# An mLSTM cell and a squared-ReLU FFN: squares moved to another engine, weights rounded two pieces at a time, odd chunks' attention put behind 64-row matmuls

## The chip, the cores and the metric

The kernel runs on one core of a Trainium2 chip. The core has a matrix engine (TensorE, PE in the profile), a vector engine (VectorE, DVE), an engine for functions of one argument (ScalarE, ACT), a general engine (GpSimd, POOL) and an engine that here only issues transfers (SyncE, SP). They run side by side, each in the order of its own instructions, and wait for each other through semaphores. SBUF is the on-chip memory, PSUM the memory that TensorE writes to, and transfers (DMA) run between DRAM and SBUF. The metric is the device time of one execution in microseconds (us), as a median over several runs.

## The reference

Two parts, one after the other. The first is an mLSTM cell: for 4 x 8 pairs of batch and head, 768 steps and a head size of 40, a matrix state and a vector state are decayed and added to at each step. The second is an FFN over 3072 tokens of width 320 with 2048 hidden units.

```python
for t in range(S):
    m_new = np.maximum(f_gate[:, :, t] + m, i_gate[:, :, t])
    f_stab = np.exp(f_gate[:, :, t] + m - m_new)
    i_stab = np.exp(i_gate[:, :, t] - m_new)
    m = m_new
    C = f_stab[:, :, None, None] * C + i_stab[:, :, None, None] * np.einsum('bhd,bhe->bhde', vt, kt)
    n = f_stab[:, :, None] * n + i_stab[:, :, None] * kt
    h_tilde = np.einsum('bhde,bhe->bhd', C, qt)
    nq = np.einsum('bhd,bhd->bh', n, qt)[:, :, None]
    denom = np.maximum(np.abs(nq), 1.0)
    o = 1.0 / (1.0 + np.exp(-o_gate[:, :, t]))
    y[:, :, t] = o * h_tilde / denom
x = y.transpose(0, 2, 1, 3).reshape(B * S, H * D)   # 3072 x 320
h = np.maximum(x @ w_in, 0.0)
out = h * h @ w_out
```

The FFN's weights come in as float64; the kernel makes float32 of them on the chip.

## The kernel before

Tokens are worked on in 24 chunks of 128 (`s` = 0 to 23; six chunks are one sequence, so chunks 0, 6, 12 and 18 start with no state). The recurrence is turned into attention inside a chunk, plus a state carried from chunk to chunk. Two chunks together make a group `g` of 256 tokens for the FFN, so there are 12 groups.

One chunk's attention is this series of steps. `load_A` brings a table of summed log decays, 512 KB, spread over all partitions, into one of two buffers. `decays` (ScalarE) makes exps of it that scale q (`scale_q`, VectorE); `mask` (POOL) blanks the future; `weigh` (ScalarE) makes eight exps, the weights; `values` (POOL) scales v for the state. `scores` (TensorE, L423) multiplies k by q with 40 rows of the array for each product, and `weighted` (VectorE, L438) multiplies scores by weights. `attend_turned` (L513, L522, L532) makes the numerator `numT` from the state and the weighted scores, and the state's increase `dC`; VectorE turns numT in blocks of 32 into `tn` and adds up the new state. Then the result goes twice through DRAM to get into the layout of the FFN: `store_num` (L551) writes `tn`, `load_num` (L556, four DMAs) reads it back, `normalise_turned` (VectorE) divides and applies the output gate, `store_rows` (L603) writes the rows, `load_rows` (L608, four DMAs) reads them as `xT`, and `turn_squares` (VectorE, L615) turns blocks of 32. `pair_up` (L289, four DMAs) and `load_squares` (L311, four DMAs) bring k and q of a later chunk in the layout for `scores`; `turn_kq` (L318) turns their blocks; `load` and `load_o` bring k, v and the output gate. All these DMAs are issued by SyncE, in the order in which the program has them.

The FFN's two products are done by a scheme with fewer multiplications (seven products of half blocks instead of eight) from group 3 on for the first product and from group 1 on for the second. `sums_of_x` (POOL) makes sums `xs` of the two chunks of a group. `ffn1_open` (L813) runs 32 matmuls: block X on xT of the group's first chunk, Y, V and Z on xs. `ffn1_close` runs 24 more over 128 rows (L813) and then 32 over 64 rows (L845), and VectorE and ScalarE join the four results; `ffn1_square` (ScalarE) takes rectifier and square in place. `ffn2_fast` (L739) is the second product in four steps of 32, 32, 32 and 16 matmuls.

The start is different. Until chunk 5 the weights are brought and rounded at the same time (`Rounding`: two reads by ScalarE, L196 and L198; three operations by VectorE, L207, L211 and L212; one add by POOL, L216). w_in takes 10 pieces of 512 columns, w_out 16 pieces of 320. Groups 0 to 2 go through `ffn1_main` and `ffn1_rest` (L645, L656), whose results `relu_half` (ScalarE, L671) writes into temporary tiles, and `square_half` (VectorE, L678) squares into the tile `g2` that the second product reads. Groups 0 and 1 are in the loop over `u`, group 2 is in the first four rounds of the main loop.

The order is written out by hand: no scheduler moves anything. The main loop (L1028) goes over quarters of chunks, `s, at = 6 + n // 4, n % 4`. Even chunks (from 8) carry the second product of group (s - 6) / 2, odd ones (from 9) the first product of group (s - 3) / 2, which holds chunks s - 3 and s - 2:

```python
    for n, (which, g, i) in enumerate(parts):
        s, at = 6 + n // 4, n % 4
        if at == 0:
            do(score, s)
        if at == 1:
            do(attend_turned, s)
```

So chunk o (odd) is attended to in its first two quarters, normalised and sent to DRAM in the third; the blocks of its xT are turned in the second quarter of chunk o + 1, `sums_of_x` reads them in its fourth, and `ffn1_open` in the first quarter of chunk o + 2.

Of the kernel before, what the change touches and what calls it, by code (L numbers as in the profile page):

```python
# [9 lines left out]
F32 = mybir.dt.float32  # L10
I32 = mybir.dt.int32
# [18 lines left out]
def kernel(  # L30
# [127 lines left out]
            ))  # L158
    IN_DONE = (3, 5, 8, 10)
    assert len(pieces) == IN_DONE[-1]  # L160
    pieces += [(w_out[:, fb, :], [(slice(0, P), wout_w[fb * P : (fb + 1) * P])]) for fb in range(NF)]
    NRAW = 4

    class Rounding:
# [11 lines left out]
        def fetch(self):  # L176
            n = len(self.raws)
            if n == len(pieces):
                return
            dst, srcs = pieces[n]  # L180
            raw = conv.tile([P, 512, 2], I32, name="raw", bufs=NRAW)
            self.raws.append(raw)
            for rows, src in srcs:
                to = raw[rows, : dst.shape[1]]
                if len(src.shape) == 4:
                    to = to.rearrange("p (a f) w -> p a f w", a=src.shape[1])
                nc.sync.dma_start(to, src)

        def words(self):
            n = len(self.a)  # L190
            if n == len(pieces):
                return
            w = pieces[n][0].shape[1]
            raw = self.raws[n][:, :w]
            mag = conv.tile([P, 512], F32, name="mag", bufs=3)
            nc.scalar.activation(mag[:, :w], raw[:, :, 1].bitcast(F32), AF.Abs)  # L196
            low = conv.tile([P, 512], F32, name="low", bufs=3)
            nc.scalar.activation(low[:, :w], raw[:, :, 0].bitcast(U32), AF.Copy, bias=2.0, scale=2.0 ** -51)  # L198
            self.a.append((mag, low))

# [464 lines left out]
    def relu_half():  # L665
        if "half" in st:
            hs, g4 = st.pop("half")
            rs = []
            for h in hs:
                rs.append(ffn.tile([P, 2, WG], F32, name="r_sb", bufs=4))  # L670
                nc.scalar.activation(rs[-1][:], h[:], AF.Relu)  # L671
            st.setdefault("relu", []).append((rs, g4))

    def square_half():
        if st.get("relu"):
            rs, g4 = st["relu"].pop(0)
            for i, r in enumerate(rs):
                nc.vector.tensor_tensor(g4[:, :, i, :], r[:], r[:], op=ALU.mult)  # L678

    def ffn2(g, j, part):  # L680
        if part == 0:
# [150 lines left out]

    def ffn1_close(g, q):
        xT, xs = st["xT", g], st["xs"]
        (X, Y, V, Z), (U2, U4) = st["f1"], st["U"]
        g4 = st["g2", g][:, 8 * q : 8 * q + 8, :].rearrange("p (n two) t -> p n two t", two=2)
        t0, t1 = slice(0, P), slice(P, 2 * P)
        blocks(X, F12, xT[:, 0, 1, :], q, False)
        blocks(Y, F21, xs[:, 2, :], q, True)
        blocks(V, WS[3], xT[:, 1, 1, :], q, True)  # L840
        lo, hi = slice(0, KR), slice(KR, 2 * KR)
        for pair in (((X, lo, xT[lo, 0, 2, :]), (Y, hi, xT[hi, 1, 2, :])), ((V, lo, xT[lo, 1, 2, :]), (Z, hi, xs[hi, 1, :]))):
            for n in range(4):
# [21 lines left out]
    def do(f, s):  # L865
        if 0 <= s < NT:
            f(s)
# [84 lines left out]
    rounding.step()  # L952


    NEXT = (5, 8, 10, 11, 13, 15, 17, 19)
    for u in range(8):
        s = 2 + u // 2
        relu_half()
# [63 lines left out]
    for g in range(1, NG):  # L1022
        parts += [(2, g, i) for i in range(4)]
        if g + 2 < NG:
            parts += [(1, g + 2, i) for i in range(4)]
    LAST = (21, 23, 25, 25, 26)
    assert LAST[-1] == len(pieces)
    for n, (which, g, i) in enumerate(parts):  # L1028
        s, at = 6 + n // 4, n % 4
        if n == 5:  # L1030
            brought.close()
            late = ctx.enter_context(tc.tile_pool(name="late", bufs=1, side="right"))
        if at == 0:
            do(score, s)
        if at == 1:
            do(attend_turned, s)
            do(decays, s + 1)
            do(mask, s + 1)
            if n > 4:
                do(turn_kq, s + 1)  # L1040
            do(decay_C, s + 1)
            if s > X_SQ:
                do(turn_squares, s - 1)
            do(store_num, s)
            do(load, s + 4)
            if 8 <= s < 20:
                load_o(s + 4)
            do(load_num, s)
            do(pair_up, s + 3)
        if 5 <= n < 8:  # L1050
            sums_of_weights(n - 5)
        if n == 6:
# [21 lines left out]
                for r in range(s + 1, min(s + 5, NT)):  # L1074
                    sigmoid(r)
        if fast:
            (ffn1_close if i % 2 else ffn1_open)(g, i // 2)
            if at == 2:
                do(scale_q, s + 1)
        elif which == 1:  # L1080
            ffn1_main(g, i)
            if i % 2 == 0:
                held = st["half"]
            else:

                both = held, st["half"]
                for more, half in enumerate(both):
                    ffn1_rest(g, i - 1 + more, half[0])
                for half in both:
                    st["half"] = half  # L1090
                    relu_half()
                    square_half()
        elif g == 0:
            ffn2(g, *divmod(i, 2))
        else:
            ffn2_fast(g, i)
        if at == 2:
            do(lambda s: weigh(s, masked=True), s + 1)
            ffn1_square()
            if n < 4:  # L1100
                do(turn_kq, s + 1)
                do(scale_q, s + 1)
            do(normalise_turned, s)
            do(store_rows, s)
            do(load_squares, s + 2)
            do(load_rows, s)
            do(load_A, s + 2)
        if at == 0:
            ffn1_square()
        if n < 5:  # L1110
# [32 lines left out]
```

## Time and profile before

| what | value |
|---|---|
| median of 11 runs | 517.78 us (516.82 to 519.33) |
| profiled execution, its own time | 518.15 us |
| its span in the profile | 516.4 us, 11946 instructions |
| TensorE busy | 505.2 us, 98% |
| VectorE, ScalarE, POOL busy | 367.7, 237.7, 113.7 us |
| TensorE busy from 0 to 127 us | 120.6 us |
| VectorE, ScalarE busy from 0 to 127 us | 104.5, 76.8 us |
| TensorE's granted clock, mean | 0.993 |
| DMA | 67.64 MB, 131 GB/s over the span |

The span runs from the first to the last instruction of one execution; the run's own time is a little longer. Busy time is given by engine. The chain of work that ended last follows the program back from its end, at each step to what released it. A list in order of time gives the start, the duration and how many instructions were merged; for a DMA it is the issue on the queue of the engine (SPq), not the transfer. Matmuls overlap, so in a merged row of the chain the duration divided by the count is the pace, shorter than one matmul's own time.

### The profile page before, as it was taken

What the parts mean: (1) busy time and instruction counts of PE and PEld (TensorE: products, weight loads), DVE (VectorE), ACT (ScalarE), POOL (GpSimd) and SP (SyncE); (2) the same over time, 40 slices, a digit from 0 to 9 for tenths busy, and PEclk for the clock granted to TensorE, in tenths of its full rate; (3) what the DMA queues carried; (4) which work ended last, traced back from release to release, by engine and by line L of the source; (5) the groups of instructions that cost most, each with busy time, mean ns of one, the idle gap of its engine ahead of it and who ended that gap; (6) DMA issues with size and microseconds to landing.
All of it is one profiled execution on the core that took longest, in us unless ns stands there. A gap on an engine that the chain in (4) does not pass through costs nothing.

```text
span 516.4 us, 11946 instructions
## 1 busy us (share of the span) xinstructions
PE 505.2 (98%) x4648; PEld 463.3 (90%) x4649; DVE 367.7 (71%) x678; ACT 237.7 (46%) x496; POOL 113.7 (22%) x146
## 2 busy tenths in 40 slices
PE   9999989999999999999999999999999999999997
PEld 4878868886698999999999999999999899999997
DVE  8588988969979776677777777668668667544441
ACT  3766667643522542572651681550771642432400
POOL 3344733233304103102112112112112103020000
PEclk9997999999999999999999999999999999999999
DMA  9999599787585776685685676785755352200000
GB/s 193 216 218 193 141 163 203 182 186 137 130 163 102 167 150 121 164 157 113 166 156 110 163 155 117 174 162 96 176 119 105 95 118 77 59 8 27 1 27 27
DMA packets 238360, 67.64 MB, mean 131 GB/s; under 512 B 185728, under 2 KB 232832, under 8 KB 238304
## 3 DMA queue, kind: packets, MB, share of 16 engines
q1 hardware_dynamic: 238208, 66.68, 61.4%
q8 instruction: 37, 0.61, 0.5%
q10 hardware_dynamic: 96, 0.20, 0.1%
q14 instruction: 19, 0.16, 0.1%
HBM read 54.56 MB, written 17.86 MB: 140 GB/s over the span
## 4 chain that ended last, share of the span: by engine, by line
PE 82%; DVE 8%; DMA 3%; ACT 2%; issue 2%; SPq 2%; POOL 0%; DVEq 0%; POOLq 0%
PE h_ps L739 32%; PE h_ps L813 21%; PE h_ps L845 7%; PE tp L423 4%; PE numT L522 3%; PE h_ps L645 3%; PE h_ps L685 3%; PE hp L461 2%; PE numT L513 2%; PE idle L880 1%; DMA A_bc<-a_rows 1%; DVE mag L211 1%; DMA num_rows<-tn 1%; PE A_ps L352 1%; SPq L311 1%
## 5 line engine op out<-in xcount | busy, mean ns | idle before, releaser
L361 POOL TENSOR_SCALAR_AFFINE_SELECT A_bc<-A_bc 128x1024 f32<-128x1024 f32 x22 | 24.7, 1123 | 213.2 <-ACT kq L371 156.8
L371 ACT ACTIVATE kq<-A_bc 64x512 f32<-64x512 f32 x30 | 18.9, 629 | 72.9 <-DMA A_bc<-a_rows 72.7
L739 PE MATMUL h_ps<-T,S 128*128 128x160 f32 x352 | 51.4, 299 | 0.0
L739 PE MATMUL h_ps<-w_out,g 128*128 128x160 f32 x336 | 49.2, 303 | 0.0
L739 PEld LDWEIGHTS h_ps<-T,S 128*128 128x128 f32 x352 | 49.0, 190 | 0.0
L385 ACT ACTIVATE A_bc<-A_bc,b_T 128x128 f32<-128x128 f32 x144 | 44.0, 389 | 7.6 <-POOL A_bc L361 7.0
L739 PEld LDWEIGHTS h_ps<-w_out,g 128*128 128x128 f32 x336 | 46.1, 190 | 1.1
L645 PE MATMUL h_ps<-xT,w_in 128*128 128x256 f32 x192 | 44.6, 387 | 0.6 <-ACT xT L624 0.6
L645 PEld LDWEIGHTS h_ps<-xT,w_in 128*128 128x128 f32 x192 | 36.2, 193 | 6.2 <-ACT xT L624 0.9
L813 PE MATMUL h_ps<-xT,w_in 128*128 128x128 f32 x288 | 40.7, 284 | 0.9 <-ACT r_sb L826 0.9
L755 DVE TENSOR_TENSOR y_sb<-y_sb,h_ps 128x160 f32<-128x160 f32 x44 | 14.0, 318 | 34.6 <-PE h_ps L739 34.6
L813 PEld LDWEIGHTS h_ps<-xT,w_in 128*128 128x128 f32 x288 | 34.9, 191 | 3.9 <-ACT r_sb L826 1.1
L813 PE MATMUL h_ps<-xs,w_in 128*128 128x128 f32 x288 | 38.0, 275 | 0.0
L826 ACT COPY r_sb<-h_ps 128x512 f32<-128x512 f32 x18 | 10.5, 584 | 58.8 <-PE h_ps L813 58.8
L845 PE MATMUL h_ps<-xT,w_in 64*128 64x128 f32 x432 | 36.9, 280 | 0.0
L845 PEld LDWEIGHTS h_ps<-xT,w_in 64*128 64x128 f32 x432 | 33.4, 187 | 2.2
L813 PE MATMUL h_ps<-xs,WS 128*128 128x128 f32 x288 | 35.1, 275 | 0.0
L813 PEld LDWEIGHTS h_ps<-xs,w_in 128*128 128x128 f32 x288 | 35.1, 192 | 0.0
L813 PEld LDWEIGHTS h_ps<-xs,WS 128*128 128x128 f32 x288 | 33.6, 192 | 0.0
L850 DVE TENSOR_TENSOR r_sb<-r_sb,h_ps 128x512 f32<-128x512 f32 x18 | 12.4, 687 | 24.4 <-PE h_ps L845 24.2
L739 PE MATMUL h_ps<-w_out,g_c 128*128 128x160 f32 x192 | 28.0, 302 | 0.0
L423 PE MATMUL tp<-kqT 40*128 40x128 f32 x384 | 27.0, 280 | 0.0
(167 smaller groups left out, 1073.4 us busy)
## 6 DMA issues: line engine op xcount, KB each, us to landing
A_bc<-a_rows SPq DMA_DIRECT2D x22, 512.0 KB, 4.7
raw<-in_moe_w_out_dram SPq DMA_DIRECT2D x16, 320.0 KB, 3.6
num_rows<-tn SPq DMA_DIRECT2D x18, 256.0 KB, 4.3
kq<-num_rows SPq DMA_DIRECT2D x72, 64.0 KB, 2.1
kqT<-kq_rows SPq DMA_DIRECT2D x34, 128.0 KB, 3.5
raw<-in_moe_w_in_dram SPq DMA_DIRECT2D x8, 512.0 KB, 5.4
kq<-in_k_dram SPq DMA_DIRECT2D x24, 160.0 KB, 4.9
va<-in_v_dram SPq DMA_DIRECT2D x24, 160.0 KB, 5.1
```

The source lines that it names most:

```text
L361: nc.gpsimd.affine_select(A[:], A[:], compare_op=ALU.is_ge, fill=-1e30, base=0, pattern=[[0, H], [1, P]], channel_multiplier=-1,)
L371: nc.scalar.activation(e[rows], st[s]["A"][0][rows, PR * i : PR * (i + 1), :], AF.Exp)
L385: nc.scalar.activation(d["W"][:, i * n + h, :], A[i][:, h, :], AF.Exp, bias=b_T[:, b, c, i * n + h : i * n + h + 1],)
L423: nc.tensor.matmul(sc[i][:, j, :], lhsT=d["kT"][rows, j, :], rhs=d["qT"][rows, j, :], start=True, stop=True,)
L522: nc.tensor.matmul(numT[i][halves[g], e, :], lhsT=va_w[s % NKQ][:, h * D1 : h * D1 + DP], rhs=d["P"][h % 2][:, h // 2, :] if s < KQ_SQ els ...
L645: nc.tensor.matmul(hs[i][:, n, :], lhsT=w_in[:, a, fb * P : (fb + 1) * P], rhs=xT[:, :, a, :], start=(n == 0 and a == 0), stop=False,)
L685: nc.tensor.matmul(o_ps, lhsT=st["g2", g][:, fb, j * P : (j + 1) * P], rhs=w_out[:, fb, :], start=(fb == 0), stop=(fb == NF - 1),)
L739: nc.tensor.matmul(to, lhsT=lhsT[:, p], rhs=rhs[:, p, :], start=(start and p == 0), stop=(p == NPAIR - 1), skip_group_check=True,)
L755: add = lambda to, a, b: nc.vector.tensor_tensor(to, a, b, op=ALU.add)
L813: nc.tensor.matmul(to[:, n, :], lhsT=lhsT[:, 4 * q + n, :], rhs=rhs, start=(start and n == 0), stop=True, skip_group_check=True,)
L845: nc.tensor.matmul(to[:, n, :], lhsT=w_in2[rows, 4 * q + n, :], rhs=rhs, start=False, stop=True, skip_group_check=True,)
L850: tt(U2[:], U2[:], Y[:], op=ALU.add)
```

## The change

There are three edits. First, groups 0 to 2: the rectifier (ScalarE) writes straight into `g2`, and one square in place over 1024 elements, on ScalarE, takes the place of two VectorE products. Second, w_out's 16 pieces become 8 of 640 columns, two blocks of rows each, with the buffers for it widened, and the counts by which the loops step (`NEXT`, `LAST`) set anew. Third, for odd chunks from 9 on (`behind`): the scores come after the 64-row matmuls of the first half of the first product, which become a function of their own (`ffn1_rows`); numT and dC come in the fourth quarter, between the 128-row and the 64-row matmuls of the second half. With them go the steps of `after_values` and `load_A`; `scale_q` of the next chunk goes to the fourth quarter. Normalising and the two DMA steps of `rows_of` go to the second quarter of the next chunk, after its own `after_values` and `load_o`, and `turn_squares` to that chunk's fourth quarter, ahead of `sums_of_x`.

```diff
--- before.py
+++ after.py
@@ -158,7 +158,13 @@
             ))
     IN_DONE = (3, 5, 8, 10)
     assert len(pieces) == IN_DONE[-1]
-    pieces += [(w_out[:, fb, :], [(slice(0, P), wout_w[fb * P : (fb + 1) * P])]) for fb in range(NF)]
+    pieces += [
+        (
+            w_out[:, fb : fb + 2, :].rearrange("p a d -> p (a d)"),
+            [(slice(0, P), wout_w[fb * P : (fb + 2) * P].rearrange("(a p) c w -> p a c w", p=P))],
+        ) for fb in range(0, NF, 2)
+    ]
+    WIDE = 2 * DM
     NRAW = 4
 
     class Rounding:
@@ -178,7 +184,7 @@
             if n == len(pieces):
                 return
             dst, srcs = pieces[n]
-            raw = conv.tile([P, 512, 2], I32, name="raw", bufs=NRAW)
+            raw = conv.tile([P, WIDE, 2], I32, name="raw", bufs=NRAW)
             self.raws.append(raw)
             for rows, src in srcs:
                 to = raw[rows, : dst.shape[1]]
@@ -192,9 +198,9 @@
                 return
             w = pieces[n][0].shape[1]
             raw = self.raws[n][:, :w]
-            mag = conv.tile([P, 512], F32, name="mag", bufs=3)
+            mag = conv.tile([P, WIDE], F32, name="mag", bufs=3)
             nc.scalar.activation(mag[:, :w], raw[:, :, 1].bitcast(F32), AF.Abs)
-            low = conv.tile([P, 512], F32, name="low", bufs=3)
+            low = conv.tile([P, WIDE], F32, name="low", bufs=3)
             nc.scalar.activation(low[:, :w], raw[:, :, 0].bitcast(U32), AF.Copy, bias=2.0, scale=2.0 ** -51)
             self.a.append((mag, low))
 
@@ -665,17 +671,14 @@
     def relu_half():
         if "half" in st:
             hs, g4 = st.pop("half")
-            rs = []
-            for h in hs:
-                rs.append(ffn.tile([P, 2, WG], F32, name="r_sb", bufs=4))
-                nc.scalar.activation(rs[-1][:], h[:], AF.Relu)
-            st.setdefault("relu", []).append((rs, g4))
+            for i, h in enumerate(hs):
+                nc.scalar.activation(g4[:, :, i, :], h[:], AF.Relu)
+            st.setdefault("relu", []).append(g4)
 
     def square_half():
         if st.get("relu"):
-            rs, g4 = st["relu"].pop(0)
-            for i, r in enumerate(rs):
-                nc.vector.tensor_tensor(g4[:, :, i, :], r[:], r[:], op=ALU.mult)
+            g4 = st["relu"].pop(0)
+            nc.scalar.activation(g4, g4, AF.Square)
 
     def ffn2(g, j, part):
         if part == 0:
@@ -832,12 +835,16 @@
 
     def ffn1_close(g, q):
         xT, xs = st["xT", g], st["xs"]
+        X, Y, V, Z = st["f1"]
+        blocks(X, F12, xT[:, 0, 1, :], q, False)
+        blocks(Y, F21, xs[:, 2, :], q, True)
+        blocks(V, WS[3], xT[:, 1, 1, :], q, True)
+
+    def ffn1_rows(g, q):
+        xT, xs = st["xT", g], st["xs"]
         (X, Y, V, Z), (U2, U4) = st["f1"], st["U"]
         g4 = st["g2", g][:, 8 * q : 8 * q + 8, :].rearrange("p (n two) t -> p n two t", two=2)
         t0, t1 = slice(0, P), slice(P, 2 * P)
-        blocks(X, F12, xT[:, 0, 1, :], q, False)
-        blocks(Y, F21, xs[:, 2, :], q, True)
-        blocks(V, WS[3], xT[:, 1, 1, :], q, True)
         lo, hi = slice(0, KR), slice(KR, 2 * KR)
         for pair in (((X, lo, xT[lo, 0, 2, :]), (Y, hi, xT[hi, 1, 2, :])), ((V, lo, xT[lo, 1, 2, :]), (Z, hi, xs[hi, 1, :]))):
             for n in range(4):
@@ -952,7 +959,7 @@
     rounding.step()
 
 
-    NEXT = (5, 8, 10, 11, 13, 15, 17, 19)
+    NEXT = (5, 8, 10, 11, 12, 13, 14, 15)
     for u in range(8):
         s = 2 + u // 2
         relu_half()
@@ -1023,30 +1030,48 @@
         parts += [(2, g, i) for i in range(4)]
         if g + 2 < NG:
             parts += [(1, g + 2, i) for i in range(4)]
-    LAST = (21, 23, 25, 25, 26)
+    LAST = (16, 17, 18, 18, 18)
     assert LAST[-1] == len(pieces)
+
+    def after_values(s):
+        do(decay_C, s + 1)
+        do(store_num, s)
+        do(load, s + 4)
+        do(load_num, s)
+        do(pair_up, s + 3)
+
+    def rows_of(s):
+        do(normalise_turned, s)
+        do(store_rows, s)
+        do(load_rows, s)
+
+    def behind(s):
+        return s > 8 and s % 2 == 1 and s < NT
+
     for n, (which, g, i) in enumerate(parts):
         s, at = 6 + n // 4, n % 4
         if n == 5:
             brought.close()
             late = ctx.enter_context(tc.tile_pool(name="late", bufs=1, side="right"))
-        if at == 0:
+        if at == 0 and not behind(s):
             do(score, s)
         if at == 1:
-            do(attend_turned, s)
+            if not behind(s):
+                do(attend_turned, s)
             do(decays, s + 1)
             do(mask, s + 1)
             if n > 4:
                 do(turn_kq, s + 1)
-            do(decay_C, s + 1)
-            if s > X_SQ:
+            if s > X_SQ and not behind(s - 1):
                 do(turn_squares, s - 1)
-            do(store_num, s)
-            do(load, s + 4)
+            if not behind(s):
+                after_values(s)
             if 8 <= s < 20:
                 load_o(s + 4)
-            do(load_num, s)
-            do(pair_up, s + 3)
+            if behind(s - 1):
+                rows_of(s - 1)
+        if at == 3 and behind(s - 1):
+            do(turn_squares, s - 1)
         if 5 <= n < 8:
             sums_of_weights(n - 5)
         if n == 6:
@@ -1074,8 +1099,19 @@
                 for r in range(s + 1, min(s + 5, NT)):
                     sigmoid(r)
         if fast:
-            (ffn1_close if i % 2 else ffn1_open)(g, i // 2)
-            if at == 2:
+            if i % 2 == 0:
+                ffn1_open(g, i // 2)
+            else:
+                ffn1_close(g, i // 2)
+                if at == 3 and behind(s):
+                    attend_turned(s)
+                ffn1_rows(g, i // 2)
+                if at == 1 and behind(s):
+                    score(s)
+                if at == 3 and behind(s):
+                    after_values(s)
+                    do(load_A, s + 2)
+            if at == (3 if behind(s) else 2):
                 do(scale_q, s + 1)
         elif which == 1:
             ffn1_main(g, i)
@@ -1100,11 +1136,14 @@
             if n < 4:
                 do(turn_kq, s + 1)
                 do(scale_q, s + 1)
-            do(normalise_turned, s)
-            do(store_rows, s)
-            do(load_squares, s + 2)
-            do(load_rows, s)
-            do(load_A, s + 2)
+            if behind(s):
+                do(load_squares, s + 2)
+            else:
+                do(normalise_turned, s)
+                do(store_rows, s)
+                do(load_squares, s + 2)
+                do(load_rows, s)
+                do(load_A, s + 2)
         if at == 0:
             ffn1_square()
         if n < 5:
```

## The prediction, made before the changed kernel ran

> **What bounds the kernel now.** I read the busy times first, then the chain of work that ended last in order of time, then SyncE's queue, then TensorE's granted clock. From the page, busy times and the chain's shares:
> ```profile
> PE 505.2 (98%) x4648; PEld 463.3 (90%) x4649; DVE 367.7 (71%) x678; ACT 237.7 (46%) x496; POOL 113.7 (22%) x146
> ...
> PE 82%; DVE 8%; DMA 3%; ACT 2%; issue 2%; SPq 2%; POOL 0%; DVEq 0%; POOLq 0%
> ```
> TensorE is idle for 11.2 us of 516.4. A change that removes no matmul can win little here, and lose as much as it makes TensorE wait. One pair of chunks (13, 14) in the chain, then a run of ffn1 that follows 128-row matmuls:
> ```profile
> 238.02 1.09 PE tp L423 x16
> 239.11 3.77 PE h_ps L813 x32
> 242.88 0.60 PE numT L513 x16
> 243.48 1.02 PE numT L522 x16
> 244.81 2.88 PE h_ps L813 x24
> 247.68 1.99 PE h_ps L845 x32
> 249.67 6.45 PE h_ps L813 x56
> 256.12 1.99 PE h_ps L845 x32
> 258.10 0.89 PE tp L423 x16
> ...
> 265.47 11.06 PE h_ps L739 x80
> ...
> 466.04 6.25 PE h_ps L813 x56
> ```
> Scores (L423) take 0.89 behind the 64-row matmuls (L845) and 1.09 behind 128-row ones; 56 matmuls of L813 take 6.25 behind 128-row ones and 6.45 behind L845. Each change of tile shape costs 0.20 us. SyncE's queue, in order of time, around chunk 15:
> ```profile
> 284.13 0.42 SPq L336 DMA_DIRECT2D A_bc<-a_rows  x1
> ...
> 285.27 0.38 SPq L551 DMA_DIRECT2D num_rows<-tn  x1
> ...
> 289.99 1.91 SPq L556 DMA_DIRECT2D kq<-num_rows  x4
> 291.94 1.20 SPq L289 DMA_DIRECT2D kq_rows<-in_k_dram  x2
> 293.19 1.23 SPq L289 DMA_DIRECT2D kq_rows<-in_q_dram  x2
> 296.00 0.38 SPq L603 DMA_DIRECT2D x_rows<-x_sb  x1
> ...
> 299.32 2.68 SPq L608 DMA_DIRECT2D xT<-x_rows  x4
> ```
> load_num (L556) stands 4.72 us behind store_num (L551), for it reads what that wrote; what is behind it in the queue stands too. From numT's last matmul (282.94) until the rows of chunk 15 are loaded this chain takes some 21 us. Now it is hidden: turn_squares takes chunk 15 at 305.94, sums_of_x at 309.35, and ffn1_open of chunk 17 begins at 316.1. TensorE's clock (the column after POOL) in the one stretch where it fell:
> ```profile
> 38.00:40.00 2.00, 0.92 (x9) 0.80 (x8) 1.97 (x4) 0.20 (x1) 0.84 (x2) 1.00 0.52 125
> 40.00:42.00 2.00, 2.00 (x13) 2.00 (x13) 1.41 (x4) 0.30 (x1) 1.66 (x2) 0.66 0.79 230
> 42.00:44.00 2.00, 2.00 (x11) 2.00 (x11) 1.35 (x3) 2.00 (x8) 0.00 (x0) 0.50 1.08 276
> ```
> After a stretch with idle time TensorE runs at half clock for about 6.8 us (by the shares 0.66, 0.50, 0.50 and 0.63 of four such windows), which loses 3.4.
>
> **What the Trainium skill says.** "TensorEngine Tiling (Array Packing)", Key Properties: changing the tiling mode drains TensorE. The trace agrees: 0.20 us each. "DMA: Bandwidth & Descriptors", Anatomy of one DMA: a semaphore wait happens on the issuing sequencer before dispatch, and a DMA has a fixed cost of about 2 us. The trace agrees: the queue stands behind L556, and x_rows' store, 2.1 us to landing, is near that price. "TensorE: Matmul & The Clock Gate", Part 1: one idle window of about 3.4 us halves the clock, and about 3.4 us of sustained work restores it. The trace shows the halving, but no long idle stretch by itself.
>
> **Part 1, squares and rounding (0 to 127 us).** VectorE loses 24 squares (L678: 11.8 + 5.7 = 17.5 us). Rounding w_out in 8 pieces of 640 for 16 of 320: three instructions of 0.400 + 0.579 + 0.492 = 1.47 us become, drawn on from the 320 and 512 rows, about 2.37; 16 x 1.47 - 8 x 2.37 = 4.6 us less. ScalarE gains 12 squares of 1024 elements at 1.04 (L862) = 12.5 and loses about 3 on rounding: 76.8 to 86 of 127 us, still under TensorE's 120.6. The squares stand among exps already now without a table load between, so none is added. POOL loses about 1 us; SyncE issues 8 DMAs fewer, of twice the size, a piece or so earlier. What this frees on TensorE: the wait of 1.85 us at 68.76 (x_sb, behind rounding and squares on VectorE) and the 1.25 at 126.92 (weighted behind four squares). What it adds: at 98.7 the last square of group 1 goes in front of the copy of xT (L624) that group 2's first matmul awaits: 1.04. Sum -2.1; bounds -6 and +5.
>
> **Part 2, TensorE's order.** Now an odd chunk takes 1.09 + 3.77 + 1.93 (0.60 + 1.02 + 0.31 for dC) + 2.88 + 1.99 + 6.45 + 1.99 = 20.1. Behind the 64-row matmuls: 3.57 + 2.68 (32 and 24 matmuls at 6.25 / 56) + 1.99 + 0.89 + 6.45 + 1.93 + 1.89 = 19.4. The last term is 1.79 or 1.99, since no row shows L845 behind numT; I take the middle. 0.7 x 8 odd chunks (9 to 23) = -5.6; bounds -6.4 and -4.8. The waits of 0.82 at 165.9 and 0.91 at 406.6 lie where the order is rebuilt: -1.7.
>
> **Part 3, what moves with it.** Odd chunk o's numT goes from the second quarter to the fourth, and its normalise_turned, store_rows and load_rows into the second quarter of the even chunk e = o + 1. In SyncE's queue they follow store_num, load, load_num, pair_up of e and load_o. turn_squares goes to e's fourth quarter, just ahead of sums_of_x, and the Y block of ffn1_open in chunk o + 2 needs that. Counted from the end of numT(o), with medians from 170 to 350 us:
> - store_num(o) at 0.55 (303.67 to 304.22), load_num(o) 3.5 later, its end with pair_up 4.74 later, load_A 0.5: 9.3.
> - numT(e) ends at 0.31 + 1.89 + 0.89 + 4.54 + 1.62 = 9.25, so store_num(e) goes at 9.8.
> - load_num(e) 4.69 later (odd chunks now, with an A load just ahead), with pair_up 4.74, load_o 0.45: 19.7.
> - store_rows(o) goes there and lands in 2.1; load_rows to its last landing 4.7 (280.72 to 285.67; 396.14 to 400.53): 26.5.
> - turn_squares 0.55, three POOL instructions of xs 1.65: 28.7.
>
> TensorE is there at 9.25 + 0.31 + 11.06 + 0.89 (X block) = 21.5. It waits 7.2 us, and nothing covers it: everything behind is in order on TensorE. Normalising does not set this: turn_kq(o + 2) behind tn(e) ends at about 12, normalise_turned(o) at 14, before 19.7. What waits behind turn_squares on VectorE (a sum S, the last add of y) is not needed before the Z block. A(o + 2) is issued at 8.8 and lands in 4.5 at about 13.3, 4 us behind numT(e) (now 2.6 to 4.1), so ScalarE's exps and POOL's vw end by about 20, still ahead of xs.
>
> Over the pairs: e = 10, 14, 16 wait 7.2; e = 12, 18 start a sequence, have no L513 (0.6 less on TensorE) and wait about 7.6; e = 20 has no load_o: 6.75; e = 22 no pair_up either: 4.3; e = 24 has no numT and no second store_num: 0.55 + 3.5 + 1.75 + 2.1 (load_num) + 1.95 (normalise) + 2.1 + 4.7 + 0.55 + 1.65 = 18.9 against 1.89 + 4.54 + 10.9 + 0.89 = 18.2: 0.7. Sum 3 x 7.2 + 2 x 7.6 + 6.75 + 4.3 + 0.7 = 48.6. From the shortest and longest gaps seen (A load and store together: 6.55; load_o up to 2.4) a wait is 5.7 to 13. Each of the six waits above 6 us should also halve the clock; the skill's 3.4 us at half clock lose 1.7, the stretch here lost 3.4, and a wait that just misses the idle window loses 0. I take 2.0, near the price, since the one stretch in the trace came after several gaps: +12; bounds 0 and +20.
>
> **Sum.** 516.4 - 2.1 - 5.6 - 1.7 + 48.6 + 12 = 567.6 span. The profiled execution's time is 518.15; the median of the runs, 517.78, is 1.4 above its span: 569.
>
> **Rivals.**
> - Late rows, but the clock stays: 569 - 12 = 557. For it: waits of 1 to 2 us at 68 and 126 left the clock alone.
> - Late rows and more: load_A(e + 2), behind the late load_rows, lands behind the next L849's turn on ScalarE, and the m1 copy and bank behind it hold TensorE another 1 to 3 us a pair, or load_o and the shared landing are at their long ends: 585 and above. For it: the 0.91 at 406.6 is this wait already.
> - Rows in time, ending faster: the queue does not hold, 28.7 - 9.8 = 18.9 us from store_num(e) to xs shrink below 21.5 - 9.8 = 11.7. Then parts 1 and 2 stand alone: 569 - 60.6 = 508. Against it: load_num's 4.69 and load_num with pair_up's 4.74 would have to vanish nearly whole, and every gap measured lies above 2.8.
> - ScalarE bounds the start: each of 12 squares delays a copy that TensorE awaits: 508 + 12.5 = 521 by itself. Against it: ScalarE itself awaits TensorE's L656 for 14.6 us there.
>
> **How the numbers follow.** Late rows with half clock 0.60 (569; its own range 552 to 588), with full clock 0.22 (557), with more behind 0.09 (592), rows in time 0.08 (508), and 0.01 for no change. Within 0.2% counts as the same, about what a measurement of this kernel can tell. Faster 0.08, same 0.01, slower 0.91. Range 543 to 590: it leaves out the fast case and the far end of the slow ones.
>
> **What would show it.** In the profile after: idle time of TensorE before L816 (the Y block, xs with WS) of 5 to 9 us in each chunk 11 to 23, released by POOL's xs, that by turn_squares, that by the DMA xT<-x_rows; pairs some 45 us apart instead of 38.5 (238.02 to 276.53), or 47 with half clock; scores in odd chunks at 0.89; clock at 0.5 behind each wait; squares on ScalarE at 1.04. A gap of under 2.8 us between store_num and load_num, or store_rows issued within 12 us of store_num(e) with rows landing before ffn1_open, would make me wrong.

## The result, and the profile after

The changed kernel takes 572.44 us (median of 12 runs, 569.70 to 577.15) where the kernel before takes 517.79 in the runs beside it: a ratio of 1.106, with a 95% interval of 1.104 to 1.108. The profiled execution took 571.18 us, its span is 569.4 us and TensorE's mean granted clock 0.957 (0.993 before). The prediction was 569.

From the page of the changed kernel, busy times and the chain's shares:

```profile
PE 509.7 (90%) x4648; PEld 469.3 (82%) x4649; DVE 341.6 (60%) x630; ACT 248.6 (44%) x492; POOL 113.0 (20%) x138
...
PE 76%; DMA 10%; SPq 4%; DVE 3%; issue 3%; POOL 2%; ACT 1%; POOLq 0%; DVEq 0%
```

The 53.0 us by which the span grew divide without a rest. TensorE is busy for 4.5 us more (509.7 against 505.2) and idle for 48.5 us more (59.7 against 11.2). The second number is nearly one row in the list of waits (engine, instruction, what it waited for: us in total, times, the longest):

```profile
PE h_ps L816 <- POOL xs L811: 49.8, 8, 9.2
DVE xT L621 <- DMA xT<-x_rows: 33.9, 8, 6.2
```

The block Y of `ffn1_open`, the first that reads `xs`, waits eight times, and VectorE's turn of the rows waits for a DMA eight times. The chain of the changed kernel around chunk 15 shows one case (start, duration; lines here are some 3 to 7 higher than in the kernel before):

```profile
318.94 0.60 PE numT L519 x16
319.54 1.02 PE numT L528 x16
320.57 0.30 PE dC L538 x16
...
328.30 0.60 PE numT L519 x16
328.89 1.02 PE numT L528 x16
...
339.65 3.62 DMA x_rows<-x_sb
...
344.68 2.10 DMA xT<-x_rows
...
347.56 0.09 POOL xs L808
347.65 1.21 issue
348.86 0.72 POOL xs L808
349.58 0.42 POOL xs L811
...
350.04 2.07 PE h_ps L816 x8
```

numT of chunk 15 is done at 320.56, its `xs` at 350.0. TensorE's list has the row of L816 at 350.04 with 7.86 us of idle time before it, so TensorE was there at 342.18. SyncE's queue in the same stretch:

```profile
321.09 0.34 SPq L557 DMA_DIRECT2D num_rows<-tn  x1
...
323.40 1.84 SPq L562 DMA_DIRECT2D kq<-num_rows  x4
...
327.87 0.53 SPq L342 DMA_DIRECT2D A_bc<-a_rows  x1
330.44 0.35 SPq L557 DMA_DIRECT2D num_rows<-tn  x1
...
334.65 1.75 SPq L562 DMA_DIRECT2D kq<-num_rows  x4
...
339.02 0.53 SPq L332 DMA_DIRECT2D og<-in_o_gate_dram  x1
339.65 0.54 SPq L609 DMA_DIRECT2D x_rows<-x_sb  x1
343.29 1.86 SPq L614 DMA_DIRECT2D xT<-x_rows  x4
```

The store of chunk 15's rows (L609) comes 18.6 us after that chunk's `store_num`, and on VectorE the rows were normalised at 333.9, 5.7 us before it. They stand in the queue behind chunk 16's `store_num`, `load_num`, `pair_up` and `load_o`. TensorE's clock after the wait (windows of 2 us; the column after POOL's is the granted clock):

```profile
351.00:353.00 2.00, 2.00 (x12) 2.00 (x11) 0.69 (x1) 0.00 (x0) 0.00 (x0) 0.50 0.58 92
353.00:355.00 2.00, 2.00 (x18) 2.00 (x18) 1.31 (x2) 0.00 (x0) 0.00 (x0) 0.91 0.81 219
```

Half clock holds from the wait to about 353.4. In the chain the 48 matmuls of L816 then take 7.33, 7.09, 7.03, 7.19, 7.66 and 7.03 us behind the six longest waits, against 5.62 where the clock stays: 9.6 us in all. TensorE's 4.5 us are these 9.6, less some 5 that were won. Of the 5 the order won some 3.4, and 1.7 come from the start, where half clock lasted 3.4 us in this execution (32.5 to 35.9) and 6.8 in that of the kernel before.

### The profile page after: what moved, and what is told of

Read it like the earlier page. It is cut to its first block, busy times and chain, and to the rows that moved or that the text cites. A ratio compares the mean times of both kernels' runs of the same rounds, so it can differ in the third digit from the quotient of the medians.

```text
span 569.4 us, 11848 instructions
## 1 busy us (share of the span) xinstructions
PE 509.7 (90%) x4648; PEld 469.3 (82%) x4649; DVE 341.6 (60%) x630; ACT 248.6 (44%) x492; POOL 113.0 (20%) x138
## 4 chain that ended last, share of the span: by engine, by line
PE 76%; DMA 10%; SPq 4%; DVE 3%; issue 3%; POOL 2%; ACT 1%; POOLq 0%; DVEq 0%
PE h_ps L742 22%; PE h_ps L816 20%; PE h_ps L651 7%; PE h_ps L852 6%; DMA x_rows<-x_sb 4%; PE tp L429 3%; PE h_ps L688 3%; PE numT L528 3%; DMA xT<-x_rows 3%; SPq L614 2%; PE h_ps L662 2%; PE hp L467 2%; PE numT L519 2%; POOL xs L808 2%; DMA num_rows<-tn 1%
## 5 line engine op out<-in xcount | busy, mean ns | idle before, releaser
L816 PE MATMUL h_ps<-xs,WS 128*128 128x128 f32 x288 | 45.3, 323 | 50.3 <-POOL xs L811 49.8
L816 PEld LDWEIGHTS h_ps<-xs,WS 128*128 128x128 f32 x288 | 42.6, 235 | 52.0 <-POOL xs L811 51.3
L367 POOL TENSOR_SCALAR_AFFINE_SELECT A_bc<-A_bc 128x1024 f32<-128x1024 f32 x22 | 26.6, 1210 | 173.9 <-ACT kq L377 156.2
L377 ACT ACTIVATE kq<-A_bc 64x512 f32<-64x512 f32 x30 | 18.8, 627 | 83.5 <-DMA A_bc<-a_rows 83.4
L651 PE MATMUL h_ps<-xT,w_in 128*128 128x256 f32 x192 | 45.9, 394 | 1.9 <-ACT xT L630 1.6
L651 PEld LDWEIGHTS h_ps<-xT,w_in 128*128 128x128 f32 x192 | 36.7, 196 | 8.3 <-ACT xT L630 2.0
L545 DVE STREAM_TRANSPOSE tn<-numT 128x256 f32<-128x256 f32 x36 | 16.0, 450 | 42.9 <-PE numT L528 42.1
L816 PE MATMUL h_ps<-xs,w_in 128*128 128x128 f32 x288 | 38.5, 277 | 1.2 <-DVE r_sb L831 1.2
L816 PE MATMUL h_ps<-xT,w_in 128*128 128x128 f32 x288 | 38.9, 278 | 0.0
L808 POOL TENSOR_TENSOR xs<-xT 128x128 f32<-128x128 f32 (+1 forms) x18 | 18.7, 1059 | 94.2 <-DVE xT L621 86.1
L852 PE MATMUL h_ps<-xT,w_in 64*128 64x128 f32 x432 | 36.9, 280 | 0.0
L816 PEld LDWEIGHTS h_ps<-xs,w_in 128*128 128x128 f32 x288 | 35.6, 195 | 1.4 <-DVE r_sb L831 1.4
L829 ACT COPY r_sb<-h_ps 128x512 f32<-128x512 f32 x18 | 10.5, 586 | 58.5 <-PE h_ps L816 58.5
L816 PEld LDWEIGHTS h_ps<-xT,w_in 128*128 128x128 f32 x288 | 35.2, 192 | 1.1
L852 PEld LDWEIGHTS h_ps<-xT,w_in 64*128 64x128 f32 x432 | 33.4, 187 | 2.0 <-issue 0.5
L621 DVE STREAM_TRANSPOSE xT<-xT 128x384 f32<-128x384 f32 x18 | 10.1, 559 | 34.3 <-DMA xT<-x_rows 33.9
```

Of the source, the lines that this page charges most:

```text
L367: nc.gpsimd.affine_select(A[:], A[:], compare_op=ALU.is_ge, fill=-1e30, base=0, pattern=[[0, H], [1, P]], channel_multiplier=-1,)
L377: nc.scalar.activation(e[rows], st[s]["A"][0][rows, PR * i : PR * (i + 1), :], AF.Exp)
L545: nc.vector.transpose(to[:, 2 * i : 2 * i + 2], numT[i][:, :2, :].rearrange("p c t -> p (c t)"))
L651: nc.tensor.matmul(hs[i][:, n, :], lhsT=w_in[:, a, fb * P : (fb + 1) * P], rhs=xT[:, :, a, :], start=(n == 0 and a == 0), stop=False,)
L808: sub = lambda to, a, b: nc.gpsimd.tensor_tensor(to, a, b, op=ALU.subtract)
L816: nc.tensor.matmul(to[:, n, :], lhsT=lhsT[:, 4 * q + n, :], rhs=rhs, start=(start and n == 0), stop=True, skip_group_check=True,)
```

## The experiments

In what follows o is an odd chunk and e the one after it. A median is given with the ratio to the kernel before on the same chip; the before medians there were 516.5 to 517.0.

**The start edits alone.** Squares and rounding as in the change, the order of the main loop as before:

```diff
-                nc.vector.tensor_tensor(g4[:, :, i, :], r[:], r[:], op=ALU.mult)
+            nc.scalar.activation(g4, g4, AF.Square)
...
+        ) for fb in range(0, NF, 2)
```

> Squares on ScalarE and w_out rounded two pieces at a time, with the order of before from chunk 6 on. Late-rows theory: nothing of the loss is here; some 514 us, since in the changed kernel the scores of chunk 8 begin 3.7 us earlier (138.29 against 142.03). Rival, that ScalarE is burdened at the start: 518 us or more.

514.16 us, ratio 0.996 (0.9943 to 0.9976). Both waits that the prediction named, 1.85 and 1.25, are gone, and 1.05 before L651 at 98.92, behind the copy of xT, has come, as its price of 1.04 said. A second series on another chip:

> The start edits alone (squares and rounding) once more, beside the two others on one chip: 514 to 514.5, ratio 0.996. The difference to the run with numT between and the joins first is the worth of the tile shapes saved.

513.63, ratio 0.9939 (0.9922 to 0.9957). So the start is worth 2.3 to 3.4 us (predicted 2.1). In this profile, as in that of the changed kernel, a wait of 1.2 us behind a rectifier on ScalarE (L675) has come where the wait of 1.85 was.

**Squares alone, rounding alone.** The first two edits of the change, one at a time:

```diff
-                rs.append(ffn.tile([P, 2, WG], F32, name="r_sb", bufs=4))
-                nc.scalar.activation(rs[-1][:], h[:], AF.Relu)
+                nc.scalar.activation(g4[:, :, i, :], h[:], AF.Relu)
...
-                nc.vector.tensor_tensor(g4[:, :, i, :], r[:], r[:], op=ALU.mult)
+            nc.scalar.activation(g4, g4, AF.Square)
```

> Only the squares of groups 0 to 2 go to ScalarE; rounding and order are those of before. By the prediction the squares free both waits of the start (1.85 and 1.25 us) and add 1.04: some 2 us of the 2.3 that both edits win, 514.5 us. If rounding makes the gain: 516.5 us.

515.56, ratio 0.9955 (0.9935 to 0.9975). By the ratio this is as much as both edits together won in the first series, by the medians it is 1.4 us; both waits are gone here too.

> Only w_out's pieces rounded two at a time. If the squares made all of the gain of the start edits: the waits of 1.85 at 68.8 and 1.25 at 126.9 stay, the same as before within 0.2 per cent (516 to 517.5). If the rounding has a share of its own (VectorE 4.6 us less work): scores start earlier, 515 to 516.

518.61, ratio 1.0031 (1.0016 to 1.0045). Neither expectation held: it is a little slower. Waits of TensorE in its profile:

```profile
PE tp L629 <- DVE x_sb L598: 4.5, 2, 3.5
PE h_ps L651 <- POOL w_in L222: 1.8, 1, 1.8
```

The wait for `x_sb` that was 1.9 at its longest is 3.5 with the squares still on VectorE, and a wait for `w_in` of 1.8 is new, while the 1.25 at 126.92 is gone. Yet `x_sb` comes only 0.33 us later (69.09 for 68.76), since TensorE was there sooner, and the span of this execution, 516.1, is not above the 516.4 of before. So these waits do not explain the 1.6 us between the medians, and that stays open. The squares win by themselves and the rounding does not; whether the rounding adds something once the squares have left VectorE, the intervals do not tell.

**The order alone.** The third edit without the first two, against the kernel before:

```diff
-        if at == 0:
+        if at == 0 and not behind(s):
             do(score, s)
...
+            if behind(s - 1):
+                rows_of(s - 1)
```

> Only the order of odd chunks is changed; squares and rounding are those of before. Late-rows theory: the whole loss is here, 572.4 + 3.7, some 576 us. If the three edits were needed together for the loss: clearly below 560 us.

573.72, ratio 1.1114 (1.108 to 1.1148); TensorE waits for `xs` 45.7 us in eight times. The whole loss lies in the order.

**TensorE kept busy during the wait.** The whole change, and ahead of the block Y of groups 4 to 10 thirty products of zeros into the bank of PSUM that Y writes to, which the block then overwrites:

```diff
+        if q == 0 and 4 <= g <= 10:
+            for _ in range(30):
+                nc.tensor.matmul(
+                    Y[:].rearrange("p a t -> p (a t)"), lhsT=zeros[:, :1].to_broadcast([P, P]),
+                    rhs=zeros[:, :1].to_broadcast([P, W]), start=True, stop=True, skip_group_check=True,
+                )
         blocks(Y, WS[1], xs[:, 3, :], q, True)
```

> The changed kernel, with 30 matmuls on zeros (about 0.216 us each, 6.5 us) put into the Y bank ahead of the Y block in the first half of groups 4 to 10, where TensorE waits. Theory that the clock falls in the wait: the clock stays full, 56 matmuls of L816 behind the wait take 6.25 to 6.45 again instead of about 7.9, and the time falls by 1.5 to 2 us a pair, to 560 to 564 us. Rival, that the wait alone is the loss: 572 us, or more where 30 matmuls are longer than the wait.

565.89, ratio 1.0945 (1.0911 to 1.0978), span 561.5, mean clock 0.994. TensorE in the same pair of chunks as above:

```profile
334.53 1.05 PE L816 MATMUL h_ps<-xT,w_in 128*128 128x128 f32 x8
335.64 6.51 PE L832 MATMUL h_ps<-zeros 128*128 128x512 bf16 x29
342.97 2.05 PE L816 MATMUL h_ps<-xs,WS 128*128 128x128 f32 x16 [0.82 <-POOL xs L811]
```

The trace has 29 of the thirty products. The sixteen matmuls behind the wait take 2.05 instead of 3.61, and pairs of chunks lie 45.6 us apart (297.40 to 342.97) instead of 47.5 (302.59 to 350.04). By the spans this wins 7.9 us, by the medians 6.5, and by the two ratios 5.9, a little less than expected. It is the worth of the half clock less a cost of the experiment: up to the block Y of group 9 it had won 10.2 us (432.33 for 442.53), and it lost 2.6 again up to that of group 10, where the wait had been 2.33 and the thirty products take 6.51. The rest of the loss is the wait itself.

**The rows taken out of the loss.** From chunk 9 on, odd chunks read as their rows those of the chunk two before, ahead of time, so that part of the output is computed from other data. All instructions and transfers stay, but the loads of the rows no longer stand behind their store, so what follows in the queue goes out sooner too:

```diff
             if behind(s):
                 do(load_squares, s + 2)
+                load_rows(s, s - 2)
```

> The changed kernel, but load_rows of an odd chunk from 9 on is issued in its own third quarter and brings the rows of the chunk two before; store_rows stays where the change puts it. So the output is another one; all work is done, and only the data that ffn1_open waits for is there early. Late-rows theory: the eight waits of TensorE on xs (49.8 us) and the half clock behind them (about 10) go, some 509 to 514 us. Rival, that scores and numT in their new places, the later load_A or the waits on ScalarE cost the time by themselves: 540 us or more.

534.68, ratio 1.0353 (1.0325 to 1.0382). The largest part of the loss goes, but it is a miss by over 20 us: TensorE still waits for `xs` 16.2 us in eight times. VectorE, just before one of these:

```profile
318.55 0.32 DVE L759 TENSOR_TENSOR y_sb<-y_sb,h_ps 128x160 f32<-128x160 f32 x1 [0.72 <-PE h_ps L743]
318.78 0.17 DVE L574 TENSOR_SCALAR dm<-kq 128x8 f32<-128x8 f32 x1
...
320.49 0.57 DVE L622 STREAM_TRANSPOSE xT<-xT 128x384 f32<-128x384 f32 x1
```

The rows lie ready, but `turn_squares(o)` (L622) stands behind `normalise_turned(e)` (L574 to L583), and this in turn behind a sum of the second product (L759) that awaits TensorE. Its own 1.7 us hold the turn; a wait for `load_num(e)` stands ahead of it only once, 0.55 us. And of these waits, far shorter, three halve the clock too. Windows of the same kernel around a wait of 2.90 us that ended at 241.24:

```profile
239.00:241.00 2.00, 0.00 (x0) 0.00 (x0) 1.01 (x2) 0.00 (x0) 2.00 (x3) 1.00 1.00 215
241.00:243.00 2.00, 1.76 (x11) 1.76 (x12) 0.18 (x1) 0.00 (x0) 0.64 (x2) 0.73 0.94 97
243.00:245.00 2.00, 2.00 (x11) 2.00 (x11) 1.06 (x2) 0.00 (x0) 0.00 (x0) 0.50 0.60 95
```

**The same, with the turn first.** `turn_squares(o)` ahead of `normalise_turned(e)` on VectorE, the rows again those of the chunk two before:

```diff
-        if at == 3 and behind(s - 1):
-            do(turn_squares, s - 1)
...
+                if behind(s - 1):
+                    do(turn_squares, s - 1)
                 do(normalise_turned, s)
```

> The kernel with the rows of the chunk two before loaded early (534.7 us, its output another one), and turn_squares of the odd chunk put ahead of normalise_turned of the even one on VectorE. Theory that what was left there is VectorE's order, turn_squares behind an operation that awaits load_num: the 16.2 us of waits on xs and some 5 us of half clock go, 509 to 513 us. Rival, that the three POOL instructions after TensorE's other work set it: 525 us or more.

522.52, ratio 1.0102 (1.0062 to 1.0142). The waits of TensorE:

```profile
PE h_ps L817 <- DVE g L859: 3.4, 3, 1.8
PE h_ps L817 <- DVE g_c L859: 2.2, 2, 1.5
...
PE h_ps L817 <- POOL xs L812: 0.4, 1, 0.4
```

The order of VectorE alone differs from the run before. The wait for `xs` is down to 0.4 us, as expected, but the time misses what was expected by over 9 us. What is left above the start edits alone, 8 us, is partly new: blocks of L817 wait for VectorE's joins, which free their PSUM bank and stand behind `turn_kq` and a late turn of rows.

**The rows first in the queue, for the whole computation.** In e's second quarter the order is now `store_num(e)`, the rows of o, and then the loads; `turn_squares(o)` ahead of `normalise_turned(e)`:

```diff
-            if not behind(s):
+            if behind(s - 1):
+                do(decay_C, s + 1)
+                do(store_num, s)
+                rows_of(s - 1)
+                do(load, s + 4)
+                do(load_num, s)
+                do(pair_up, s + 3)
+            elif not behind(s):
                 after_values(s)
```

> The changed kernel, complete, with store_rows and load_rows of the odd chunk put behind store_num of the even one and ahead of its load, load_num and pair_up in SyncE's queue, and turn_squares ahead of normalise_turned on VectorE. Late-rows theory: store_rows goes out about 6 us earlier, the waits on xs fall from 8 us to about 2 a pair, and a new wait of some 3 us a pair comes in behind load_A of the even chunk, which goes out later: 540 to 552 us. Were the queue not what holds the rows: 565 us or more.

539.44, ratio 1.0439 (1.0396 to 1.0483). SyncE's queue of that kernel:

```profile
354.26 0.35 SPq L557 DMA_DIRECT2D num_rows<-tn  x1
357.77 0.36 SPq L609 DMA_DIRECT2D x_rows<-x_sb  x1
359.83 1.85 SPq L614 DMA_DIRECT2D xT<-x_rows  x4
```

Between `store_num(e)` (L557) and the store of the rows (L609) lie 3.51 us for 9.21 in the changed kernel, and between that and their load (L614) 2.06 for 3.64. What is left of the first is VectorE's: the rows are normalised at 357.74. The waits for `xs` are down to 2.9 us, and the time is just under what was expected: 33 of the 55 us are won back by the queue and one turn. What remains has moved. VectorE:

```profile
375.59 1.25 DVE L324 STREAM_TRANSPOSE kqT<-kqT 128x1024 f32<-128x1024 f32 x1 [3.86 <-DMA kqT<-kq_rows]
377.68 0.58 DVE L621 STREAM_TRANSPOSE xT<-xT 128x384 f32<-128x384 f32 x1 [0.83 <-DMA xT<-x_rows]
378.18 0.65 DVE L857 TENSOR_TENSOR r_sb<-r_sb,h_ps 128x512 f32<-128x512 f32 x1
378.75 0.67 DVE L858 TENSOR_TENSOR g_c<-r_sb,h_ps 128x512 f32<-128x512 f32 x1
```

Two turns await DMAs and the joins stand behind them; TensorE waits for these 10.1 us in six times, and for L831, which frees another bank, 7.3 in seven.

**And the joins first.** The same, with `turn_kq(o + 1)` behind the joins and scores of the second quarter and `turn_squares(o - 1)` behind the joins of the fourth:

```diff
-            if n > 4:
+            if n > 4 and not behind(s):
                 do(turn_kq, s + 1)
...
                     score(s)
+                    do(turn_kq, s + 1)
```

> The whole change with the rows first in SyncE's queue and turn_squares(o) ahead of normalise_turned(e), as in the run at 539.4, and now in odd chunks turn_kq(o+1) behind the joins and the weighted scores of the second quarter and turn_squares(o-1) behind the joins of the fourth. If the joins (L857 to L860) that stand behind these two turns, which await DMAs, hold TensorE there: its waits on g and g_c (10.1 us in 6) go, and with them 2 to 4 us of half clock behind them, 525 to 529; the waits of the block L816 on r_sb (7.3 us in 7) are ScalarE's and may stay. If the joins are late for another reason (the copies on ScalarE behind exps that await A_bc): 536 to 540. Below 517 would need both to go, and is not expected.

540.81, ratio 1.0429 (1.0389 to 1.0469): no gain, where 525 to 529 was expected. The waits for g and g_c are gone, and another has their place; besides, half clock came more often in this profile, with a mean clock of 0.978 for 0.994. ScalarE of this kernel:

```profile
380.57 1.27 ACT L377 ACTIVATE kq<-A_bc 64x512 f32<-64x512 f32 x2 [13.47 <-DMA A_bc<-a_rows]
381.86 0.60 ACT L856 ACTIVATE g_c<-h_ps 128x512 f32<-128x512 f32 x1
382.35 0.58 ACT L829 COPY r_sb<-h_ps 128x512 f32<-128x512 f32 x1
```

and its waits of TensorE:

```profile
PE h_ps L816 <- ACT r_sb L829: 9.2, 4, 2.6
PE h_ps L816 <- DVE r_sb L831: 8.3, 7, 1.9
```

The exps of the next table of decays (L377) await `load_A`, issued at 376.26 behind `load_rows(e)`, and the copies that free TensorE's banks (L829) stand behind them. An order with `load_A` earlier was not tried.

**The gain of the order by itself.** With the start edits, numT and dC alone of an odd chunk go between the 128-row and the 64-row matmuls, in the quarter where they were; scores and rows stay:

```diff
+        between = which == 1 and g > 2 and s < NT
...
                 ffn1_close(g, i // 2)
+                if at == 1 and between:
+                    attended()
+                ffn1_rows(g, i // 2)
```

> Squares and rounding as changed; of the order, only this: numT and dC of odd chunks from 9 on go between the 128-row and the 64-row matmuls of the same quarter, 2.7 us later than before, and scores, normalising and all DMAs stay in their quarters. Two changes of tile shape fewer a chunk, 0.2 to 0.4 us, 1.6 to 3.2 us over 8 chunks: against 514.2 us without it, 511 to 512.6 us. If 2.7 us already bring the rows late: above 514 us.

518.33, ratio 1.0017 (0.9997 to 1.0037): slower than the start edits alone, where a gain was expected. The rows are in time, for no wait names `xs`, and the order of all other engines and of the transfers is that of the start edits alone. A chunk without a wait takes 19.58 us (315.16 to 334.74) against 19.78 (311.80 to 331.58) with the start edits alone, so the 0.20 is real. But five times a block L816 waits 0.86 for a join. VectorE then:

```profile
245.91 0.62 DVE L551 TENSOR_TENSOR C<-dC,Cd 40x164 f32<-40x164 f32 x2
246.57 1.25 DVE L324 STREAM_TRANSPOSE kqT<-kqT 128x1024 f32<-128x1024 f32 x1
247.74 0.54 DVE L621 STREAM_TRANSPOSE xT<-xT 128x384 f32<-128x384 f32 x1
248.31 0.69 DVE L857 TENSOR_TENSOR r_sb<-r_sb,h_ps 128x512 f32<-128x512 f32 x1
248.91 0.68 DVE L858 TENSOR_TENSOR g_c<-r_sb,h_ps 128x512 f32<-128x512 f32 x1
```

numT comes 2.7 us later, and with it everything that VectorE has to do between numT and the joins. So the two turns, which nobody awaits soon, were put behind the joins:

```diff
+        def attended_rest():
+            if n > 4:
+                do(turn_kq, s + 1)
...
+            if s > X_SQ:
+                do(turn_squares, s - 1)
...
                 ffn1_rows(g, i // 2)
+                if at == 1 and between:
+                    attended_rest()
```

What else stands in `attended_rest` keeps its place in the order of its own engine, so against the run before only the two turns move.

> Squares and rounding as in the change, numT and dC of odd chunks between the 128-row and the 64-row matmuls of the second quarter, and on VectorE the turns of k, q and of the squares set behind the joins of that quarter. If the waits of 0.86 us (join L857 and L858 before the block L816) come from these two turns standing ahead of the joins, they are gone: five waits of 0.86 less 4.3 us than with numT between alone, 512 to 513.5, and below the start edits alone (514.2) by up to 8 x 0.20 = 1.6. If they come from tn and C instead, which stay ahead of the joins, the waits stay and the time is 516 to 518.

512.74, ratio 0.9925 (0.9907 to 0.9944), and the waits for the joins are gone. This beats the kernel before and the changed one. Against the start edits alone on the same chip, 0.9939 (0.9922 to 0.9957), it is 0.9 us less, of 1.6 that the tile shapes could give; the intervals overlap, so the order's own gain is not shown.

## Why the prediction was right, step by step

**Part 3, late rows.** Counted from the end of numT(15), each step as predicted and as the changed kernel has it:

| step | predicted | measured |
|---|---|---|
| store_num(o) | 0.55 | 0.53 |
| load_num(o), later by | 3.5 | 2.31 |
| load_num(o) to load_A | 4.74 | 4.47 |
| store_num(e), at | 9.8 | 9.88 |
| load_num(e), later by | 4.69 | 4.21 |
| load_num(e) to load_o | 4.74 | 4.37 |
| store_rows(o), at | 19.7 | 19.09 |
| store_rows to load_rows | 2.1 | 3.64 |
| load_rows to the turn | 4.7 | 3.60 |
| turn and xs | 2.2 | 3.10 |
| xs ready, at | 28.7 | 29.4 |
| TensorE there, at | 21.5 | 21.6 |
| wait | 7.2 | 7.86 |

The mechanism and its sum hold: eight waits of 49.8 us against 48.6, singly 8.34, 9.23, 8.27, 7.86, 7.96, 5.46, 2.33 and about 0.3 against 7.2, 7.6, 7.2, 7.2, 7.6, 6.75, 4.3 and 0.7. That the sum is this near is in part luck, for errors of its terms cancel: waits for e up to 18 were up to 1.6 longer, those for e = 20 to 24 shorter. Four terms were mis-sized. The store of the rows was priced as in the kernel before; behind `pair_up` and `load_o` it took 3.02 to 4.31 us from L609 to L614 (e = 10 to 18), 2.31 behind `pair_up` alone (e = 20), and 2.14 and 2.07 with neither (e = 22, 24). With the rows first it was 2.06 to 2.08 in seven pairs of eight. `num_rows` landed sooner (2.31 for 3.5), and the landing of the rows was 1.1 shorter.

The first of these gaps also answers a sign that the prediction had set for being wrong, less than 2.8 us between `store_num` and `load_num`. It did appear: for the odd chunks 9 to 21 the gap was 2.13 to 2.31. It changed nothing, for behind this load the queue had time to spare. `load_A` went out at 327.87, and `store_num(e)` only at 330.44, when numT(e) was there; the gaps of `load_num(e)`, which do count, were 3.0 to 5.2 up to e = 20.

The fourth is `xs`: 1.65 became 2.45. VectorE's sum S lies over the two subtractions of the odd chunk's part:

```profile
347.40 1.18 DVE L737 TENSOR_TENSOR S<-S,g 128x1024 f32<-128x1024 f32 x1
347.55 2.02 POOL L808 TENSOR_TENSOR xs<-xT 128x128 f32<-128x128 f32 x2 [11.13 <-DVE xT L621]
```

The first of the two took 1.34 us and ended 0.31 behind the sum; with the rows first it takes 0.45. The Trainium skill, "SBUF — State Buffer", Who interferes with whom, says this: a `tensor_tensor` on VectorE with both inputs in SBUF and a GpSimd operation that reads SBUF exclude each other, and the later one blocks fully. The trace agrees: the run with the rows first, where that sum does not lie there, has the two subtractions in 1.14 us instead of 2.02. The prediction had passed over that sum as harmless.

**Normalising "does not set this".** True of `normalise_turned(o)`, done 5.7 us before its store. But `turn_squares(o)` stands behind `normalise_turned(e)` as well, which the prediction did not say; with the rows early its place there, and the sum S that then lies over `xs`, keep 16.2 us of waits. It cost nothing in the pair of the table, where the rows came 5.6 us later still.

**Half clock.** 12 predicted, 9.6 in the blocks, six waits as said; 2.0 each was 1.4 to 2.0, so the 1.7 that the prediction had passed over was nearer. Kept busy, TensorE won 5.9 to 7.9 us back, and 10.2 before the products of zeros themselves began to cost. The rival "late rows, but the clock stays" falls.

**Parts 1 and 2.** Start -2.1, measured -2.3 and -3.4. Order -0.7 a chunk: with TensorE kept busy an odd chunk without a wait takes 0.89 + 5.36 + 1.99 + 0.89 + 6.45 + 1.93 + 1.99 = 19.5 against 20.1, so 0.6, since L852 behind numT takes 1.99, the upper of the two values. Where a wait stands ahead of the block Y, 0.26 of it is lost again, for the 48 matmuls then take 5.62 at full clock and not 5.36. The old waits of 0.82 and 0.91 are gone, but 1.2 before L816 (r_sb) and 0.5 (g) are new. The sum of 567.6 fell 1.8 short of the span of 569.4: +1.2 from the waits for `xs`, -2.4 from the half clock, +0.5 from the rest of TensorE's busy time (-5.1 for -5.6, of which -1.7 is the half clock at the start and only -3.4 the order) and +2.5 from TensorE's other idle time, which is 1.3 less than before (48.5 - 49.8) where 3.8 less was expected. So the total, too, is nearer than its terms. The median stands 3.0 above the profiled span, where 1.4 was added.

**The rivals.** "Late rows and more", A(e + 2) late behind the late `load_rows`, did not act in the changed kernel: no wait of TensorE names it. Its mechanism is real, though: with the rows and the joins early it holds TensorE for 9.2 us in four waits. "Rows in time" did not happen, and the runs show that it would not have given 508: the rows made ready gave 534.7, and with the turn early 522.5, because the next thing is late behind the first. ScalarE did not bound the start: the squares on it alone gain, though its rectifier can cost 1.2 us there.

## What to carry over

When work moves past a transfer queue issued in order, time it by the queue: each load that reads what a store in front of it wrote holds all that is behind it, and here such steps cost up to 9.2 us a pair where the better order of matmuls won 0.6 a chunk. A wait removed is worth what stands next in line: here queue, turn, joins and table of decays lay one behind the other, and putting the joins first won nothing for the 10.1 us of waits that it took away. Before a producer is moved later on TensorE, list what the other engines have between it and the step that frees the next bank, and put what nobody awaits soon behind that step.

## What the hardware showed that was not expected

- Half clock after short waits. In the run with the rows ready, waits of 2.90, 2.05 and 2.44 us (ended at 241.24, 323.62 and 364.97) were followed by sixteen matmuls in 3.18, 3.60 and 3.59 us, while behind waits of 2.05, 2.33, 2.05 and 2.05 (201.06, 283.38, 406.74, 446.98) they took about 2.05. The Trainium skill, "TensorE: Matmul & The Clock Gate", Part 1, names an idle window of about 3.4 us; here 2.05 was enough in one case and not in the others, so the measurement decides: such a wait may or may not halve the clock. What tells the seven cases apart can be worked out from the granted clock in this trace. It falls at 241.93, 323.85 and 364.81, each time for 3.41 us, and these times lie 81.92 and 40.96 apart, which is 24 and 12 times 3.413: in this trace the clock changes in whole steps of 3.41 us. In the step just ahead of a fall TensorE was busy for 0.69, 1.36 and 1.14 us. In the other four cases the end of a step cut the wait in two, and no step held less than 1.45 (1.45, 1.58, 2.33, 1.61). So among these seven not the length of the wait decided but how it lay in the steps. Busy time in a step is not the whole rule, though: in the run with the turn first a step with 1.9 busy was followed by half clock.
- The landing of one and the same store, 192 KB: 2.06 us with no load issued just ahead of it, 3.02 to 4.31 behind loads of k, q and the output gate. Which of these loads delays it was not taken apart.
- A change of tile shape is worth 0.20 us also where numT is moved by itself (19.58 for 19.78 a chunk).
